# Adding the attention softmax's 1e-9 on ScalarE, as a bias behind the exponentials, instead of on VectorE ahead of the reciprocal

## The chip, the cores and the metric

The kernel runs on one core of a Trainium2 chip. The metric is the time of one execution on the device in microseconds (us); lower is better. The profile comes from one execution of the same program, recorded by the hardware.

## What is computed

Four batches of eight heads of causal attention with a window of 64 positions, then two feed-forward layers. Cut to what matters here:

```python
B, H, S, D = 4, 8, 576, 64
scores = np.where(mask, q @ k.T / np.sqrt(D), -1e9)       # 0 <= row - column < 64
scores = scores - np.max(scores, axis=-1, keepdims=True)
attn = np.exp(scores)
attn = attn / (np.sum(attn, axis=-1, keepdims=True) + 1e-09)
x = attn @ v                       # 2304 tokens x 512
h = x @ w_in                       # 512 x 2048
g = np.where(h >= 1, h, np.where(h <= -1, 0, (h + 1) ** 2 / 4))
x = g @ w_out                      # 2048 x 512
# second layer: h = x @ w_in2 (512 x 1024), h * softmax(h), layer norm, @ w_out2
```

The largest term of every softmax row is exp(0) = 1, so each sum is at least 1.

## The kernel before, in words

**Attention.** The 2304 tokens are cut into 12 tiles of 192 rows, each tile into three blocks of 64 queries that see 128 keys each. A unit of attention is two heads of one tile. The scores of a unit come out of TensorE into PSUM (`st_s`, L352); VectorE adds the mask and takes the maximum (L360); ScalarE makes three exponentials, one for each block, with the maximum as bias and the row sum as accumulator output (L366, each an ACTIVATE with an ACTIVATION_READ_ACCUMULATOR behind it). The three sums of a unit lie side by side in `sm` (128 x 3). `st_norm` adds 1e-9 to them on VectorE, in place (L377), takes the reciprocal into `rs` (L378) and multiplies the 128 x 384 probabilities `p` with it (L386; in a sequence's first tile L382 for the first block and L386 for the other two). `st_t` transposes `p` on TensorE (L400, L402) and ScalarE copies it to SBUF (L405, L407); `st_v` multiplies by v (L421) and splits the result into a high and a low part (`xh` on ScalarE, L428, `xl` on VectorE, L429). The first 18 units are done one at a time like this; the other 30 go in 15 pairs (`pair_s`, `pair_v`), with the same steps under L442, L452, L458, L476, L483 and L484, and `st_norm` is then called twice in a row. In all `st_norm` runs 48 times.

**First layer.** For each of six blocks of 384 tokens there are 16 steps f. A step multiplies `xh` and `xl` with the high and low parts of w_in into `ps_h` (L496, 12 matmuls), applies the activation (`u`: Relu with a bias tile `half` at L505, Square at L506, both ScalarE; L511 VectorE), splits `u` into `gh` (L512, ScalarE) and `gl` (L515, VectorE), and, two steps later, adds the product with w_out to four accumulators (L526, 12 matmuls). `moe_out` copies these out at a block's end (L536 ScalarE, L538 VectorE).

**Weights.** They arrive in HBM as 64-bit numbers. In the first block they are loaded through five staging buffers `wst` (L124, L126; the first ones by SyncE's queue, the others by GpSimd's), and each is turned into a high and a low part in three stages, one per call of `w_conv`: L132 (ScalarE), L136 and L137 (VectorE), L145 (ScalarE) and L146 (VectorE). L146 is the last reader of a staging buffer: the next load waits for it.

**Order.** A main loop runs over the steps f. The attention of later tokens is a generator, `slots()`, from which each step takes one or two pieces; a prologue (ahead of `slots`) does the first seven units by hand. The instructions are not issued in the order in which the program is traced: when the program is built, a planner goes through them with estimated durations and gives each engine, of those that it takes to be ready, the one traced first. On the chip each engine then works through its own queue in that fixed order. A changed instruction can thus move others.

Of the kernel before, what the change touches and what calls it, by code (L numbers as in the profile page):

```python
# [8 lines left out]
F32 = mybir.dt.float32  # L9
F32R = mybir.dt.float32r  # L10
U32 = mybir.dt.uint32
ACTF = mybir.ActivationFunctionType
ALU = mybir.AluOpType
# [7 lines left out]
def kernel(  # L21
# [12 lines left out]
    nc = tc.nc  # L34
# [21 lines left out]
    const = ctx.enter_context(tc.tile_pool(name="const", bufs=1))  # L56
# [8 lines left out]

    make_identity(nc, ident)
    nc.vector.memset(half, 0.5)
    nc.vector.memset(mhalf, -0.5)
    nc.gpsimd.memset(mask, 0.0)
    for x in range(2):  # L70
# [270 lines left out]
    def first(t, i):  # L341
        return t % TPB == 0 and i == 0
# [29 lines left out]
    def st_norm(g, u=None):  # L372
        t = (g if u is None else 2 * g) // NP
        u = g if u is None else (g, u)
        p, sm = pr[u], sums.pop(u)
        rs = at_p.tile([128, QB], F32, tag="rs", name="rs")
        nc.vector.tensor_scalar(sm, sm, 1e-9, None, op0=ALU.add)  # L377
        nc.vector.reciprocal(rs, sm)  # L378
        eng = nc.vector
        i0 = 0  # L380
        if first(t, 0):
            eng.tensor_tensor(  # L382
                p[:, 0, 64:], p[:, 0, 64:], rs[:, 0:1].to_broadcast([128, 64]), op=ALU.mult
            )
            i0 = 1
        eng.tensor_tensor(  # L386
            p[:, i0:, :], p[:, i0:, :],
            rs[:, i0:].rearrange("p (i o) -> p i o", o=1).to_broadcast([128, QB - i0, 128]),
            op=ALU.mult,
        )  # L390
# [172 lines left out]
    for n in range(G0 + 4):  # L563
        if n <= G0:
            st_s(n)
        if 1 <= n <= G0 + 1:
            st_norm(n - 1)
        if 0 <= n - 2 <= G0:
            st_t(n - 2)
        if n == NQ:  # L570
            after(load_qk, 2 * NP)
        if n == NV:
            after(load_v, 2)
        if n + 2 <= G0 + 1:
            st_qkt(n + 2)
        if 0 <= n - 3 < G0:
            st_v(n - 3)
        if n >= NC:
            w_conv()
            w_load(1)  # L580
# [19 lines left out]
    def slots():  # L600
        for g in range(G0 + 1, GB + 1):
            st_s(g)
            yield
            st_v(g - 1)
            st_norm(g)
            yield
            qkt_and_loads(g + 1)
            v_ahead(g)
            yield
            st_t(g)  # L610
            if g == GB:
                st_s(g + 1)
            yield
        st_norm(GB + 1)
        qkt_and_loads(2 * PU)
        yield
# [378 lines left out]
```

## Time and profile before

| | us |
|---|---|
| median of 3 runs | 706.09 (705.32 to 706.83) |
| the profiled execution | 703.17 |
| its span, first to last instruction | 701.4 |
| busy in the span: TensorE matmul, VectorE, ScalarE, GpSimd | 678.1, 448.3, 412.5, 134.2 |

The profile names engines PE (TensorE matmul), PEld (TensorE weight load), DVE (VectorE), ACT (ScalarE), POOL (GpSimd) and SP (SyncE); a q behind the name is that engine's queue of DMA issues. L377 is line 377 of the kernel. An arrow `out<-in` names what is written and what is read. A wait is idle time of the waiting engine, put down to what ended it.

### The profile page before, as it was taken

To read this page: it belongs to the slowest core of one execution; us is meant where nothing else is said; L and a number is where in the kernel's file an instruction comes from. 1 tells how busy PE (TensorE), PEld (TensorE's weight loads), DVE (VectorE), ACT (ScalarE), POOL (GpSimd) and SP (SyncE) were. 2 spreads that over 40 slices of the span, in tenths; PEclk is the share of its full clock that TensorE was granted. 3 is DMA by queue.
4 is the path that set the end of the run, shared out by engine and by line. 5 is a ranking of instruction groups with operands and counts; after the bars stand their busy time and mean duration, and the time that the engine had idled before them with its cause. 6 is when DMAs were issued, how large, how long until landed. Compare 5 with 4: busy or idle time off the path is not lost.

```text
span 701.4 us, 12574 instructions
## 1 busy us (share of the span) xinstructions
PE 678.1 (97%) x4439; PEld 625.6 (89%) x4439; DVE 448.3 (64%) x1213; ACT 412.5 (59%) x1006; POOL 134.2 (19%) x178
## 2 busy tenths in 40 slices
PE   6899888899999999999999999999999999999998
PEld 5689788799999999999999999999997888888887
DVE  4789889646445555454455552643289999999850
ACT  5889777665656655665566565364455555445451
POOL 1112221100001000021112111662272322220000
PEclk9999999999999999999999999999999999999999
DMA  9996896625353523346351211562024455444331
GB/s 194 253 241 161 218 245 196 148 35 108 72 116 112 116 64 76 77 129 126 85 113 61 106 41 51 173 202 93 1 83 142 155 178 189 158 147 150 103 109 46
DMA packets 150551, 88.94 MB, mean 127 GB/s; under 512 B 118616, under 2 KB 134744, under 8 KB 150488
## 3 DMA queue, kind: packets, MB, share of 16 engines
q1 hardware_dynamic: 135160, 49.84, 30.2%
q0 software_dynamic: 12592, 33.57, 14.9%
q10 hardware_dynamic: 2736, 4.72, 1.8%
q8 instruction: 35, 0.57, 0.3%
q14 instruction: 28, 0.23, 0.1%
HBM read 63.97 MB, written 24.12 MB: 126 GB/s over the span
## 4 chain that ended last, share of the span: by engine, by line
PE 71%; issue 13%; POOL 4%; DVE 4%; DMA 3%; SPq 3%; ACT 2%; POOLq 0%; DVEq 0%
PE acc L526 21%; PE ps_h L496 21%; PE ps_o L827 14%; PE P L712 9%; DMA wst<-in_moe_w_in_dram 3%; POOL wil L249 2%; PE ps_x L476 2%; PE ps_s L442 2%; PE ps_p L402 2%; SPq L279 1%; DVE gl L515 1%; POOL wst L124 1%; SPq L302 1%; POOL wst L126 1%; DVE x2p L692 1%
## 5 line engine op out<-in xcount | busy, mean ns | idle before, releaser
L511 DVE SCALAR_TENSOR_TENSOR u<-u,ps_h 128x384 f32<-128x384 f32 (+1 forms) x98 | 53.3, 544 | 142.3 <-ACT u L506 141.4
L496 PE MATMUL ps_h<-xh,wih 128*128 128x384 f32 (+1 forms) x392 | 132.0, 337 | 3.1 <-ACT wih L145 3.0
L526 PE MATMUL acc<-gl,woh 128*128 128x384 f32 (+1 forms) x392 | 130.3, 334 | 2.1 <-DVE gl L515 2.1
L496 PE MATMUL ps_h<-xl,wih 128*128 128x384 f32 (+1 forms) x392 | 130.7, 334 | 0.4 <-DVE xl L429 0.4
L496 PE MATMUL ps_h<-xh,wil 128*128 128x384 f32 (+1 forms) x392 | 130.9, 334 | 0.0
L526 PE MATMUL acc<-gh,wol 128*128 128x384 f32 (+1 forms) x392 | 129.3, 332 | 0.0
L526 PE MATMUL acc<-gh,woh 128*128 128x384 f32 (+1 forms) x392 | 123.8, 341 | 2.3 <-ACT gh L512 2.3
L505 ACT ACTIVATE u<-ps_h,half 128x384 f32<-128x384 f32 (+1 forms) x98 | 56.1, 574 | 97.5 <-PE ps_h L496 97.3
L515 DVE TENSOR_TENSOR gl<-u,gh 128x384 fp32r<-128x384 f32 (+1 forms) x98 | 62.6, 640 | 35.2 <-ACT gh L512 34.6
L512 ACT CAST gh<-u 128x384 fp32r<-128x384 f32 (+1 forms) x98 | 49.7, 508 | 49.9 <-DVE u L511 34.8
L496 PEld LDWEIGHTS ps_h<-xh,wih 128*128 128x128 f32 x392 | 74.1, 189 | 4.5 <-ACT wih L145 3.6
L526 PEld LDWEIGHTS acc<-gh,woh 128*128 128x128 f32 x392 | 72.0, 188 | 6.2 <-ACT gh L512 3.5
L526 PEld LDWEIGHTS acc<-gl,woh 128*128 128x128 f32 x392 | 73.7, 188 | 3.1 <-DVE gl L515 2.7
L496 PEld LDWEIGHTS ps_h<-xl,wih 128*128 128x128 f32 x392 | 74.1, 189 | 1.0 <-DVE xl L429 0.8
L496 PEld LDWEIGHTS ps_h<-xh,wil 128*128 128x128 f32 x392 | 74.1, 189 | 0.1
L526 PEld LDWEIGHTS acc<-gh,wol 128*128 128x128 f32 x392 | 73.6, 188 | 0.1
L712 PE MATMUL P<-wih,x2p 128*128 128x512 f32 x216 | 71.6, 390 | 0.7 <-DVE x2p L692 0.7
L827 PE MATMUL ps_o<-woh,wol 128*128 128x512 f32 (+1 forms) x152 | 57.6, 379 | 0.0
L827 PE MATMUL ps_o<-woh,woh 128*128 128x512 f32 (+1 forms) x152 | 57.5, 379 | 0.0
L827 PE MATMUL ps_o<-wol,woh 128*128 128x512 f32 (+1 forms) x152 | 57.5, 378 | 0.0
L506 ACT ACTIVATE u<-u 128x384 f32<-128x384 f32 (+1 forms) x98 | 51.1, 522 | 1.9
L712 PEld LDWEIGHTS P<-wih,x2p 128*128 128x128 f32 x216 | 40.4, 188 | 9.2 <-DVE x2p L692 1.1
(123 smaller groups left out, 1191.8 us busy)
## 6 DMA issues: line engine op xcount, KB each, us to landing
wst<-in_moe_w_out_dram POOLq DMA_DIRECT2D x22, 512.0 KB, 7.4
wst<-in_moe_w_in_dram POOLq DMA_DIRECT2D x21, 512.0 KB, 5.5
vw<-in_v_dram SPq DMA_DIRECT2D x32, 256.0 KB, 5.3
lnd<-e SPq DMA_DIRECT2D x16, 512.0 KB, 2.7
lT<-lnd SPq DMA_DIRECT2D x64, 128.0 KB, 3.0
x2d<-xo POOLq DMA_DIRECT2D x24, 192.0 KB, 2.6
out_dram<-o ACTq DMA_DIRECT2D x17, 256.0 KB, 2.0
w2d<-w2st POOLq DMA_DIRECT2D x8, 512.0 KB, 3.0
```

Source lines behind the costliest of these rows:

```text
L249: nc.gpsimd.tensor_tensor(lo, v_, as_f32(hi), op=ALU.subtract)
L402: nc.tensor.transpose(ps[:, i * 128:i * 128 + 128], p[:, i, :], ident)
L442: nc.tensor.matmul(ps[x][64 * c:64 * c + 64, i * 128 + c0:i * 128 + 128], z[r, KQ + i * 64:KQ + i * 64 + 64], z[r, i * 64 + c0:i * 64 + 12 ...
L496: nc.tensor.matmul(ps, a, bb[:, kc, c], start=(n == 0), stop=(n == 3 * KC - 1))
L505: nc.scalar.activation(u, ps, ACTF.Relu, bias=half, scale=0.5)
L506: nc.scalar.activation(u, u, ACTF.Square)
L511: g = nc.vector.scalar_tensor_tensor(u, u, 1.0, ps, op0=ALU.min, op1=ALU.max)
L512: return nc.scalar.copy(hi, u).ins, g.ins
L515: nc.vector.tensor_tensor(lo, u, as_f32(hi), op=ALU.subtract)
L526: nc.tensor.matmul(acc[j, e][:, c], a, bb, start=(f == 0 and n == 0 and c.start == 0), stop=(f == NF - 1 and n == 2),)
L712: nc.tensor.matmul(ps, l, r, start=(n == 0), stop=(n == 5))
L827: nc.tensor.matmul(ps, a[kk // 4][:, kk % 4, :], b[kk][:, c:c + w], start=(n == 0), stop=(n == 3 * NK2 - 1),)
```

## The change

A 128 x 1 tile `eps` is filled with 1e-9 by VectorE at the start. In `st_norm`, the addition on VectorE becomes a Relu on ScalarE, in place, with `eps` as bias. The softmax of the second layer (L770) is left as it is.

```diff
     make_identity(nc, ident)
     nc.vector.memset(half, 0.5)
+    eps = const.tile([128, 1], F32, name="eps")
+    nc.vector.memset(eps, 1e-9)
     nc.vector.memset(mhalf, -0.5)
...
         rs = at_p.tile([128, QB], F32, tag="rs", name="rs")
-        nc.vector.tensor_scalar(sm, sm, 1e-9, None, op0=ALU.add)
+        nc.scalar.activation(sm, sm, ACTF.Relu, bias=eps, scale=1.0)
         nc.vector.reciprocal(rs, sm)
```

## Rows read from the trace of the kernel before

**Rows 1.** Busy time by stretch: start and end, length, then PE, PEld, DVE, ACT, POOL.
```profile
0.00:40.00 40.00, 31.67 (x229) 26.72 (x229) 25.26 (x113) 28.29 (x101) 5.31 (x16) 0.96 1.03 221
40.00:140.00 100.00, 90.56 (x652) 84.34 (x652) 84.51 (x247) 76.60 (x201) 18.26 (x29) 1.00 0.80 202
140.00:440.00 300.00, 300.00 (x2322) 290.86 (x2318) 153.41 (x487) 179.77 (x469) 36.03 (x52) 1.00 0.37 89
```

**Rows 2.** The waits of PE up to 140 us: total us, times, longest us.
```profile
PE ps_p L402 <- DVE p L386: 3.7, 2, 2.4
PE ps_h L496 <- ACT wih L145: 3.0, 2, 1.6
...
PE acc L526 <- ACT gh L512: 2.3, 4, 1.3
PE ps_s L352 <- ACT kq L339: 2.0, 4, 1.0
```

**Rows 3.** Busy time by stretch of line 377 alone (x instructions).
```profile
0.00:20.00 20.00, 0.74 (x4) 1.00 1.05 197
20.00:140.00 120.00, 2.29 (x14) 0.99 0.83 209
```

**Rows 4.** Groups of instructions by line and shape: busy us, mean ns of one, idle before.
```profile
L458 ACT ACTIVATE p<-p,mx 128x128 f32<-128x128 f32 x82 | 31.8, 390 | 12.2 <-DVE mx L452 12.2
...
L377 DVE TENSOR_SCALAR sm<-sm 128x3 f32<-128x3 f32 x48 | 7.4, 156 | 2.0 <-ACT p L366 1.2 <-ACT p L458 0.5
...
L458 ACT ACTIVATE p<-p,mx 128x64 f32<-128x64 f32 x8 | 2.7, 342 | 0.2 <-DVE mx L452 0.2
...
L338 ACT ACT_TABLE_LOAD x1 | 1.3, 1283 | 0.7 <-PEq L979 0.7
```

**Rows 5.** Timeline from 31.2 us: start, length, engine, line, operation [idle before <-releaser].
```profile
31.20 0.19 ACT L366 ACTIVATION_READ_ACCUMULATOR p<-p,mx 128x1 f32 x1
...
31.29 0.68 ACT L132 ACTIVATE wst<-wst 128x512 f32<-128x512 f32 x1
...
31.62 0.16 DVE L377 TENSOR_SCALAR sm<-sm 128x3 f32<-128x3 f32 x1
31.82 0.18 DVE L378 RECIPROCAL rs<-sm 128x3 f32<-128x3 f32 x1
...
32.73 0.69 PE L402 MATMUL ps_p<-ident,p 128*128 128x128 f32 x3 [1.37 <-DVE p L386]
```

**Rows 6.** Timeline from 145 us: two dependent instructions of ScalarE.
```profile
145.19 0.58 ACT L505 ACTIVATE u<-ps_h,half 128x384 f32<-128x384 f32 x1 [0.30 <-PE ps_h L496]
...
145.81 0.53 ACT L506 ACTIVATE u<-u 128x384 f32<-128x384 f32 x1
```

**Rows 7.** Waits up to 120 us: GpSimd's weight loads for line 146.
```profile
POOL wst L126 <- DVE wil L146: 23.3, 8, 15.8
```

**Rows 8.** Timeline: a pair's last multiplication, and the first transposes that read the pair.
```profile
145.70 0.56 DVE L386 TENSOR_TENSOR p<-p,rs 128x384 f32<-128x384 f32 x1
...
151.58 0.60 PE L402 MATMUL ps_p<-ident,p 128*128 128x128 f32 x4
```

**Rows 9.** Timeline from 131.8 us.
```profile
131.89 0.19 ACT L366 ACTIVATION_READ_ACCUMULATOR p<-p,mx 128x1 f32 x1
131.98 0.46 ACT L536 COPY xo<-acc 128x384 f32<-128x384 f32 x1
...
132.31 0.17 DVE L378 RECIPROCAL rs<-sm 128x3 f32<-128x3 f32 x1
...
133.23 0.52 PE L402 MATMUL ps_p<-ident,p 128*128 128x128 f32 x3 [2.35 <-DVE p L386]
```

**Rows 10.** The chain that ended last, in order of time: start, us, what.
```profile
20.57 10.68 DMA wst<-in_moe_w_in_dram
```

**Rows 11.** Timeline: one unit of the first block, addition and multiplication.
```profile
73.57 0.16 DVE L377 TENSOR_SCALAR sm<-sm 128x3 f32<-128x3 f32 x1
...
79.91 0.55 DVE L386 TENSOR_TENSOR p<-p,rs 128x384 f32<-128x384 f32 x1
```

## The prediction

> **What bounds the kernel now.** I read the busy times by stretch first. The reader is to see that from 140 to 440 us TensorE is busy for all of its 300 us, while VectorE has 153 and ScalarE 180 [rows 1]: there, nothing that these two do a little sooner or later moves the end. Ahead of 140 us it is not so: TensorE stands still for 8.3 us up to 40 us and for 9.4 us from 40 to 140, and in that second stretch VectorE is busy 85% and ScalarE 77% of the time. So I read the waits of TensorE up to 140 us next [rows 2]. It waits for VectorE's normalized `p` twice (3.7 us in all) and for ScalarE's products (`wih`, `gh`, `kq`) ten times (7.3 us). The change touches the first kind directly, and the second through what it puts into ScalarE's queue. Then I read where the 48 additions lie: 4 up to 20 us, 14 from there to 140 [rows 3], so the other 30, two for each of 15 pairs, lie behind 140 us. The second layer's softmax is not touched, so the end of the kernel is out of reach except by a new order.
>
> **The removed addition.** 48 instructions of 156 ns on VectorE, 7.4 us of busy time [rows 4]. Where the reciprocal follows directly it starts 0.20 us after the addition started (31.62, 31.82) [rows 5]: that is what VectorE gains each time.
>
> **The added Relu.** No row shows an ACTIVATE on three columns, so I bound it. Below: an accumulator read, 0.19 us [rows 5]. Above: the narrowest Exp, 64 columns, 342 ns. That Exp also reads its bias from a 128 x 1 tile, and 64 more columns cost it 390 - 342 = 48 ns [rows 4], so three columns give 342 - 61 x 0.75 = 296 ns, 0.30 us. I take this, since engine, memory and kind of bias are the same. Relu, Exp, Square, Copy and Prelu already run with one table load in the whole trace [rows 4], so no second load comes with it.
>
> **Its wait.** The Relu reads what the third accumulator read has written, on its own engine. An independent instruction starts 0.10 us before such a read ends (31.29 against 31.39) [rows 5], a dependent one 0.04 us after its predecessor's end (145.81 against 145.77) [rows 6]. So the Relu costs ScalarE 0.30 + 0.04 = 0.34 us where nothing fills the gap, as the overlap lost ahead of it is won back behind it; 48 times are 16 us, and they are a price only where ScalarE is late. The reciprocal, which used to follow on VectorE's own queue, now waits across engines. Queued behind it are the multiplication and, in the first block, the weight conversion, and GpSimd's weight loads wait for its last step, L146, 23.3 us in eight waits [rows 7].
>
> **The memset of `eps`.** One instruction of 128 x 1 at the start, ahead of the first transposes' results, when VectorE has nothing to do: nothing. With that cover gone it costs less than an addition, under 0.16 us.
>
> **The 30 units behind 140 us.** Hidden: the pair shown ends its last multiplication at 146.26 and its transposes start at 151.58 [rows 8]; 5.3 us of cover stand against a delay of 0.1 to 0.6 us for each unit, and TensorE is full. Nothing. With the cover gone each would cost what the two places below do.
>
> **Place A, 31 us.** TensorE waits 1.37 us for `p`. The sums are ready at 31.39; VectorE adds at 31.62 and takes the reciprocal at 31.82 [rows 5]. With the Relu first in ScalarE's queue it runs from 31.43 to 31.73, and with 0.04 us of handing over the reciprocal starts at 31.77: 0.05 us earlier. Behind L132, which ends at 31.97 and lets the next start 0.10 us sooner, it runs from 31.87 to 32.17 and the reciprocal starts at 32.21: 0.39 us later. I take the middle, +0.2 us.
>
> **Place B, 132 us.** TensorE waits 2.35 us. Sums ready at 132.08, reciprocal at 132.31 [rows 9]. Relu first: 132.12 to 132.42, reciprocal at 132.46, +0.15 us. Behind the copy L536 (131.98 to 132.44): 132.34 to 132.64, reciprocal at 132.68, +0.37 us. Middle: +0.25 us. From 140 us on TensorE has no idle time to make this up.
>
> **The other 16 early units.** The four up to 20 us hide behind transfers: the chain that ended last runs through a load issued at 20.57 that lands at 31.25 [rows 10]. For the twelve others the addition mostly has no hurry: the one at 73.57 has its multiplication at 79.91 [rows 11], 6.3 us later, since the planner put other work of VectorE between them. So the Relu is done in time, and what is left is occupancy: +0.34 us for ScalarE, -0.20 us for VectorE, each worth something only where that engine is what TensorE or a weight load waits for. Bounds: all twelve on ScalarE's path, +4.1 us; all on VectorE's, -2.4 us. TensorE's waits speak for ScalarE [rows 2], GpSimd's for VectorE [rows 7]; nearly even, so I take +0.2 us.
>
> **Sum.** 0.2 + 0.25 + 0.2 = +0.65 us. The profiled execution took 703.17 us (span 701.4 and 1.77 around it); it would take 703.8. The median of the runs is 2.92 us above the profiled one, and I put the same difference on it: 706.09 + 0.65 = **706.7 us**.
>
> **Rival 1, slower: ScalarE's queue sets the pace of the first 140 us.** The Relu stands in an in-order queue that is 77% busy from 40 to 140 us and for whose products TensorE waits ten times [rows 1, 2]. Each one that lies ahead of an L145, L512 or L339 that is already late costs 0.34 us, and where the planner puts it behind an L132 (0.68 us) the reciprocal and all that VectorE has behind it stand too. With half of the twelve on that path (2.0 us) and A and B at their upper ends (0.39 + 0.37): +2.8 us, **708.9**. It decides once four Relus are on the path (1.4 us). For it: the waits for ScalarE are TensorE's largest. Against it: ScalarE is idle for 23 us of those 100. The Trainium skill (ScalarE: Activation LUTs, section Rules for kernel authors) has this as a rule: Relus and additions belong on VectorE, not on ScalarE. By that rule this rival is the forecast; the trace agrees as far as the single operation goes, and shows for most units that nobody waits for it.
>
> **Rival 2, faster: VectorE sets the pace of the weight conversion.** From 40 to 140 us it is the busiest engine but TensorE [rows 1], and GpSimd's loads wait for its L146 [rows 7]. If each addition taken out brings the loads 0.20 us forward, twelve give 2.4 us; with A at its lower end and B at +0.15 it is -2.3 us, **703.8**. Against it: most of TensorE's waiting is for ScalarE.
>
> **Rival 3: a new order.** The planner sees another engine and other durations, and neighbours in the first 140 us change places; that it interleaves freely there shows in the 6.3 us between an addition and its multiplication [rows 11]. The size is that of one or two waits of TensorE, whose longest are 1.0 to 1.6 us [rows 2], in either direction: 704.5 to 708.9.
>
> **How the numbers follow.** The runs shown spread by 0.2% (1.5 us), so a difference under 0.2%, 1.4 us, can't be told from none. The forecast has 0.46, rival 1 0.24, rival 2 0.12, and rival 3 0.18, which I split into 0.10 slower and 0.08 faster. So faster 0.20, same 0.46, slower 0.34. The forecast's own range is 705.4 to 707.5; the range reaches to rival 1 and most of rival 2 and takes in the bounds of A and B: 704.4 to 709.2.
>
> **What would show it.** Right: 48 Relus of about 0.30 us on `sm` and no addition; the stretch from 140 to 440 us full on TensorE again; the two waits for `p` there and 0.1 to 0.4 us longer; the end of the first block later by under 1.4 us. Rival 1 would show as longer waits of TensorE for `wih`, `gh` and `kq` and new waits of VectorE for `sm`; rival 2 as weight loads that are issued earlier. I would be wrong altogether if the time changed behind 440 us, where no attention is left: that could only come from a new order there.

## The result, and the profile after

The changed kernel takes 708.55 us (median of 9 runs, 706.78 to 711.46), the kernel before took 704.43 beside it (9 runs, 703.57 to 706.83): a ratio of 1.0058, 95% interval 1.0042 to 1.0074. It is slower by 4.1 us, where the prediction had +0.65 and called the time the same. The profiled execution took 708.55 us with a span of 706.8, against 703.17 and 701.4 before. One execution of a kernel told of further down (the waits filled, with the Relu) took 1115.18 us at a mean granted clock of 0.564, where its other eleven had 0.993 to 1.000, and is left out of every figure.

The change itself is there as written. The groups of instructions by line and shape (busy us, mean ns of one, idle before) and the waits of VectorE in the changed kernel, where all lines behind the new two stand two further down (L377 is L379, L386 is L388):

```profile
L379 ACT ACTIVATE sm<-sm,eps 128x3 f32<-128x3 f32 x48 | 12.9, 290 | 0.1
L69 DVE MEMSET eps<- 128x1 f32 x1 | 0.1, 59 | 0.0
DVE rs L380 <- ACT sm L379: 13.9, 17, 1.6
```

48 Relus of 290 ns (0.30 us was estimated), a memset of 59 ns, and a new wait of the reciprocal for ScalarE, 17 times. The busy times by stretch, which answer to [rows 1]:

```profile
0.00:40.00 40.00, 30.95 (x191) 26.43 (x192) 22.82 (x97) 27.63 (x98) 5.29 (x16) 0.92 0.92 223
40.00:140.00 100.00, 91.96 (x646) 86.82 (x646) 83.17 (x241) 76.95 (x211) 18.64 (x29) 0.95 0.74 192
140.00:440.00 300.00, 299.99 (x2325) 289.94 (x2325) 147.90 (x460) 184.72 (x506) 32.38 (x47) 1.00 0.38 90
```

From 140 to 440 us TensorE is as full as before, so what was lost was lost ahead of that. But TensorE does not stand still longer in the first 140 us: 9.05 + 8.04 = 17.1 us, against 8.3 + 9.4 = 17.7 before. Its waits there, which answer to [rows 2], first those for what the two engines make:

```profile
PE ps_p L404 <- DVE p L388: 4.1, 3, 2.1
PE ps_p L404 <- ACT woh L147: 2.8, 1, 2.8
PE ps_s L354 <- ACT kq L341: 2.0, 3, 1.3
PE ps_h L498 <- DVE xl L431: 1.6, 2, 1.1
PE acc L528 <- ACT gh L514: 1.2, 2, 0.6
```

The waits of `ps_p` for the normalized `p` have grown from 3.7 us to 6.9, with a new one of 2.8 at 52 us. The waits for `wih` (3.0 us before) are gone: with TensorE later, the weights are in time. So the sum of the waits hides the loss. What shows it is the sixth number behind the length in the same view by 10 us, the clock that TensorE was granted (1.00 is 2.4 GHz, 0.50 is 1.2). The kernel before:

```profile
30.00:40.00 10.00, 8.54 (x82) 7.51 (x81) 8.01 (x26) 9.07 (x31) 1.84 (x3) 0.83 0.88 169
40.00:50.00 10.00, 9.01 (x89) 8.41 (x88) 8.16 (x32) 8.80 (x30) 1.31 (x2) 1.00 1.05 272
50.00:60.00 10.00, 10.00 (x77) 9.72 (x77) 9.28 (x27) 9.47 (x26) 2.06 (x3) 1.00 0.56 166
130.00:140.00 10.00, 7.61 (x71) 6.61 (x71) 6.54 (x25) 5.87 (x21) 2.17 (x5) 1.00 0.94 234
```

The changed kernel:

```profile
30.00:40.00 10.00, 7.25 (x50) 6.21 (x51) 8.37 (x27) 8.59 (x26) 1.84 (x3) 0.69 0.77 163
40.00:50.00 10.00, 9.23 (x92) 8.57 (x91) 8.18 (x29) 7.54 (x22) 1.30 (x2) 0.96 0.85 249
50.00:60.00 10.00, 6.69 (x41) 6.00 (x40) 9.54 (x27) 9.49 (x29) 2.87 (x4) 0.66 0.87 241
130.00:140.00 10.00, 7.20 (x48) 6.55 (x47) 5.96 (x26) 4.92 (x22) 2.71 (x5) 0.83 0.65 166
```

A mean of 0.83 over 10 us is a third of it at half clock. In the trace, TensorE ran at half clock for 3.4 us before (32.9 to 36.4), and for 6.8 (33.9 to 40.7), 6.8 (51.0 to 57.8) and 3.4 us (136.3 to 139.7) after. Before, the stretch lies behind the first of the two waits for `p`, and none behind the longer second. After, the first and the third begin inside a wait for `p`; the second begins 1.0 us ahead of the wait of 2.8 us, behind waits of 0.8 and 0.5 us. What a stretch costs is read from TensorE's own rows at the two levels, start and length, in the changed kernel:

```profile
34.08 0.88 PE L404 MATMUL ps_p<-ident,p 128*128 128x128 f32 x3 [1.68 <-DVE p L388]
36.27 0.41 PE L498 MATMUL ps_h<-xh,wil 128*128 128x192 f32 x1
36.48 0.42 PE L498 MATMUL ps_h<-xh,wih 128*128 128x192 f32 x1
41.20 0.28 PE L498 MATMUL ps_h<-xl,wih 128*128 128x192 f32 x1
41.31 0.28 PE L498 MATMUL ps_h<-xh,wil 128*128 128x192 f32 x1
```

At half clock these matmuls start 0.21 us apart, at full clock 0.11. So half of TensorE's busy time in such a stretch is lost. Two more things had changed. The order that the planner gives is another: place by place in the two traces, and with the moved operation left out, TensorE's queue names another instruction at 556 places, VectorE's at 267 and ScalarE's at 211, the first at 17 us. And a new wait stands at 52 us, in unit 8 (units are numbered from 0 in the order of the work; place A of the prediction is unit 6, place B unit 16). ScalarE and VectorE there, in the changed kernel:

```profile
50.81 0.20 ACT L368 ACTIVATION_READ_ACCUMULATOR p<-p,mx 128x1 f32 x1
50.91 0.68 ACT L134 ACTIVATE wst<-wst 128x512 f32<-128x512 f32 x1
51.48 0.67 ACT L147 CAST wih<-wst 128x512 fp32r<-128x512 f32 x1
52.02 0.32 ACT L379 ACTIVATE sm<-sm,eps 128x3 f32<-128x3 f32 x1
...
52.50 0.68 DVE L148 TENSOR_TENSOR wil<-wst,wih 128x512 fp32r<-128x512 f32 x1
53.10 0.16 DVE L380 RECIPROCAL rs<-sm 128x3 f32<-128x3 f32 x1
53.19 0.65 DVE L139 SCALAR_TENSOR_TENSOR wst<-wst 128x512 uint32<-128x512 uint32 x1
53.77 0.41 DVE L138 TENSOR_SCALAR wst<-wst 128x512 uint32<-128x512 uint32 x1
54.10 0.54 DVE L388 TENSOR_TENSOR p<-p,rs 128x384 f32<-128x384 f32 x1
```

The sums are ready at 51.01. The Relu stands behind two conversions and runs from 52.02 to 52.34; the reciprocal stands behind VectorE's own conversion L148, which ends at 53.18; `p` is ready at 54.64, and the transposes, which had waited since 51.99, start at 54.79. The profile names `woh` (L147) as what ended this wait, since that instruction ended at 54.80; it is `p`.

### The profile page after: what moved, and what is told of

It is laid out like the page before. It is cut to its first block, busy times and chain, and to the rows that moved or that the text cites. A ratio compares the mean times of both kernels' runs of the same rounds, so it can differ in the third digit from the quotient of the medians.

```text
span 706.8 us, 12558 instructions
## 1 busy us (share of the span) xinstructions
PE 684.3 (97%) x4439; PEld 632.5 (89%) x4439; DVE 440.5 (62%) x1166; ACT 420.1 (59%) x1054; POOL 134.5 (19%) x178
## 5 line engine op out<-in xcount | busy, mean ns | idle before, releaser
L528 PE MATMUL acc<-gh,woh 128*128 128x384 f32 (+1 forms) x392 | 128.4, 342 | 1.2 <-ACT gh L514 1.2
L514 ACT CAST gh<-u 128x384 fp32r<-128x384 f32 (+1 forms) x98 | 49.7, 509 | 49.3 <-DVE u L513 33.9
```

Source lines behind the costliest of these rows:

```text
L514: return nc.scalar.copy(hi, u).ins, g.ins
L528: nc.tensor.matmul(acc[j, e][:, c], a, bb, start=(f == 0 and n == 0 and c.start == 0), stop=(f == NF - 1 and n == 2),)
```

## The experiments

Three things were mixed: the Relu, the order, and the clock. To part them, an order can be fixed: a function ties each engine's instructions one behind the other, in an order taken from one of the two kernels.

```diff
+def pin_order(tc):
+    want = json.loads(zlib.decompress(base64.b85decode(_ORDER)))
...
+        for a, b in zip(order, order[1:]):
+            tc.add_manual_dep(b, a.name, info, reason="order")
```

**Relu in the order of before** (each Relu directly behind its third Exp).

```diff
+        pin_order(tc)
```

> The changed kernel's instructions, but each engine's queue tied to the order that it has in the kernel before; each Relu stands directly behind its unit's third exponential. Theory A (the planner's new order makes the loss): ratio to the kernel before 0.999 to 1.002, the stretch at half the TensorE clock near 51 us and the one near 136 us are gone, and the only half-clock stretch ahead of 600 us is the one near 33 us, 3.4 us long. Theory B (the Relu itself makes it, by its 0.29 us on ScalarE and the handing over to VectorE): ratio 1.004 to 1.008, as the change measured. Theory C (both about evenly): 1.002 to 1.004.

Measured: 708.82 us (6 runs, 707.96 to 710.57), ratio 1.0064 [1.0048, 1.0080].

**The add in the order of after** (the kernel before, each add directly ahead of its reciprocal).

```diff
+        pin_order(tc)
```

> The mirror image: the kernel before with its addition on VectorE, but each queue tied to the order that it has in the changed kernel, the addition directly ahead of its reciprocal. Theory A: ratio 1.004 to 1.008, with TensorE waiting 2 to 3 us for the transposes near 52 us and near 135 us and the clock at half behind each. Theory B: 0.998 to 1.002. Theory C: 1.002 to 1.004.

Measured: 709.21 us (6 runs, 708.88 to 710.21), ratio 1.0070 [1.0055, 1.0084]. Unit 8 in this kernel, VectorE and then TensorE:

```profile
52.33 0.68 DVE L146 TENSOR_TENSOR wil<-wst,wih 128x512 fp32r<-128x512 f32 x1
52.93 0.15 DVE L377 TENSOR_SCALAR sm<-sm 128x3 f32<-128x3 f32 x1
53.12 0.18 DVE L378 RECIPROCAL rs<-sm 128x3 f32<-128x3 f32 x1
...
54.82 0.87 PE L402 MATMUL ps_p<-ident,p 128*128 128x128 f32 x3 [3.43 <-DVE p L386]
```

The sums are ready at 50.85, but the add and the reciprocal stand behind the same conversion, and TensorE waits 3.43 us without any Relu, against 2.80 with it. So the wait at unit 8 comes from the place of these instructions in VectorE's queue, that is, from the new order; the Relu's 1.0 us behind ScalarE's conversions cost nothing there. The half clock comes with the order too: 10.2 us from 31.3, 6.8 from 51.8 and 3.4 from 137.1 us.

**The Relu in the first 18 units only**, order left to the planner.

```diff
-        nc.scalar.activation(sm, sm, ACTF.Relu, bias=eps, scale=1.0)
+        if not isinstance(u, tuple):
+            nc.scalar.activation(sm, sm, ACTF.Relu, bias=eps, scale=1.0)
+        else:
+            nc.vector.tensor_scalar(sm, sm, 1e-9, None, op0=ALU.add)
```

> The Relu in the 18 units that are done one at a time, the addition on VectorE in the 15 pairs; order left to the planner. All theories put the loss ahead of 150 us: ratio 1.004 to 1.007, the lag against the kernel before 4 to 5 us at 150 us and unchanged from there. If the 30 units behind 150 us carry a share by themselves, the ratio is under 1.003.

Measured: 708.50 us (6 runs, 707.53 to 709.90), ratio 1.0057 [1.0042, 1.0073].

**The Relu in the 15 pairs only**: the same edit with the two branches exchanged.

> The Relu in the 15 pairs alone, the addition on VectorE in the first 18 units; order left to the planner. Expected ratio 0.999 to 1.002: hidden under a full TensorE from 140 to 440 us, at most the 0.5 us that the changed kernel loses near 400 us. Over 1.003 would say that the prediction's cover for these units does not hold.

Measured: 704.18 us (12 runs, 702.22 to 708.18), ratio 0.9990 [0.9973, 1.0006].

What follows: the pairs are hidden, and the whole loss comes from the first 18 units. But the Relu without the new order loses 0.64%, the new order without the Relu 0.70%, and both together 0.58%: they don't add up, so neither is a price by itself. In the order of before, place by place, the two traces show it. The waits at A and B are nearly those of before, 1.34 us (1.37) and 2.48 us (2.35), but the lag behind the kernel before grows by 1.6 us at 23 to 25 us, by 1.2 behind A and by 3.4 at B (0.8 of that in a wait for the next unit's products, which before did not have). TensorE at B in this kernel, against 0.52 us for the transposes and 0.83 for the scores at the same place before:

```profile
136.21 0.87 PE L404 MATMUL ps_p<-ident,p 128*128 128x128 f32 x3 [2.48 <-DVE p L388]
136.88 1.49 PE L354 MATMUL ps_s<-kq 128*128 128x128 f32 x6
```

And at 23 us, where both kernels have waited 0.4 us, the kernel before:

```profile
22.77 0.94 PE L352 MATMUL ps_s<-kq 128*128 128x128 f32 x6 [0.38 <-ACT kq L339]
23.54 0.27 PE L400 MATMUL ps_p<-ident,p 128*64 128x128 f32 x1
```

and the Relu in the same order:

```profile
22.79 1.65 PE L354 MATMUL ps_s<-kq 128*128 128x128 f32 x6 [0.37 <-ACT kq L341]
24.23 0.42 PE L402 MATMUL ps_p<-ident,p 128*64 128x128 f32 x1
```

The same work starts at the same time and takes 0.7 us more. TensorE begins every profiled execution at half clock; the trace has no clock record for this (the column prints 1.00), but the matmuls show it. They run at full clock from 22.7 us on before, from 26.4 here, from 27.1 in the changed kernel. That is not the Relu's doing alone: see the last section.

From the traces I added up, up to the 501st product matmul of the first layer (`acc`, at 256.7 us before): TensorE's idle time, and its busy time at half clock, the start included. Half of the latter is the loss:

| kernel | starts at | idle | busy at half clock | half of it | the rest |
|---|---|---|---|---|---|
| before | 256.7 | 17.8 | 20.2 | 10.1 | 228.8 |
| after | 261.7 | 17.1 | 34.5 | 17.2 | 227.3 |
| Relu, old order | 263.1 | 18.5 | 31.6 | 15.8 | 228.7 |
| add, new order | 262.0 | 20.7 | 24.1 | 12.0 | 229.3 |
| Relu in singles | 261.7 | 16.1 | 36.3 | 18.2 | 227.4 |
| Relu in pairs | 259.3 | 17.3 | 25.9 | 12.9 | 229.1 |

The rest agrees within 2 us over all six. So in the profiled executions it is the half clock that tells the three slow Relu kernels from the one before (+5.7 to +8.1 us), not the idle time (-1.7 to +0.7); only the add in the new order has more idle time as well (+2.9). Part of this is the start, which varies by itself (last section); behind the start, the loss at half clock is 1.7 us before and 5.6 to 8.5 in the four slow kernels. The granted clock of every execution is on record too, its start apart. Its mean is 0.992 to 0.994 in the kernel before (17 to 35 executions beside each experiment), 0.991 with the Relu in the old order (6), but 0.987 in the changed kernel (9) and 0.986 with the add in the new order (6): the lower clock goes with the new order, with or without the Relu. But such a table can take company for cause. The **clock theory** says that the loss is TensorE's speed behind its waits for `p`; its rival, that it is the lateness of `p` itself. The next runs take the half clock away and leave `p` as late as it is.

**The waits filled, with the Relu and with the add, in the order of before.** Matmuls whose product nobody reads stand ahead of the transposes, in the unused last quarter of the same bank:

```diff
+FILL = {('p', 6): 5, ('p', 16): 9}
...
+    def fillers(site, ps):
+        for _ in range(FILL.get(site, 0)):
+            i = nc.tensor.matmul(ps[:, 384:512], ident, ident, start=True, stop=True)
+            FILLERS.add(i.ins.name)
...
         ps = at_bank("ps_p")
+        fillers(("p", u), ps)
         o = at_p.tile([128, QB, 128], F32, tag="pT", name="pT")
```

> relu_old_order (Relu on ScalarE, every engine in the order of before) with matmuls that nobody reads (ident by ident, 128 columns, into the unused last quarter of the bank) on TensorE directly ahead of the transposes that wait for p: 5 in unit 6 (the wait of 1.34 us at 33 us) and 9 in unit 16 (2.48 us at 134 us). Of the 6.3 us that relu_old_order lost by its profile, about 4.6 came behind these two waits, where the granted clock stood at 0.5 for 6.83 us each. Clock theory: the waits are filled, the clock stays at full speed behind them, and most of those 4.6 us come back: ratio to before 0.998 to 1.002 (703.5 to 706.0 us). Rival, the wait for p itself: p comes no earlier, the loss stays: ratio 1.004 to 1.008 (707.5 to 710 us).

> The kernel before in its own order with the same 5 and 9 unread matmuls ahead of the same two waits. Clock theory: before has one half-clock stretch of 3.41 us behind the first wait in its profile, and its runs spread over 4 us, so some of that comes back: ratio 0.996 to 1.000. Against relu_fill_waits it says how much of Relu against add is left once both waits are filled: at most 0.5 us of difference by the clock theory (the 0.2 us by which p comes later, twice), 4 us by the rival, which expects 1.000 here.

Measured: the Relu 704.64 us (11 runs, 703.50 to 705.67), ratio 0.9989 [0.9973, 1.0005], down from 1.0064 without the fillers. The add 702.73 us (12 runs, 700.36 to 704.91), ratio 0.9962 [0.9946, 0.9978], faster than either kernel. TensorE at A and B with the Relu, and the stretches around them:

```profile
33.32 1.38 PE L315 MATMUL ps_p<-ident 128*128 128x128 f32 x10
34.59 0.52 PE L412 MATMUL ps_p<-ident,p 128*128 128x128 f32 x3
...
132.82 1.84 PE L315 MATMUL ps_p<-ident 128*128 128x128 f32 x15
134.69 0.52 PE L412 MATMUL ps_p<-ident,p 128*128 128x128 f32 x3
135.05 0.83 PE L361 MATMUL ps_s<-kq 128*128 128x128 f32 x6
```

```profile
30.00:40.00 10.00, 8.95 (x92) 7.55 (x91) 8.89 (x31) 9.90 (x34) 1.56 (x3) 1.00 0.89 158
130.00:140.00 10.00, 8.98 (x79) 7.99 (x78) 5.35 (x22) 5.47 (x21) 2.72 (x5) 1.00 0.91 223
```

`p` is ready 1.13 us after its sums, as without the fillers; the transposes take 0.52 us in place of 0.87, the clock stays at 1.00 in these stretches (in this profile it is at half from 20.9 to 27.7 and from 92.5 to 95.9 us), and the ratio falls by 0.75%. That is the clock theory's number. Its other one was missed: the Relu still stands 1.9 us above the add, not 0.5. For the same fillers take 0.38% off the add as well. So of the 0.64% by which the Relu is slower than the add in this order, 0.27% is left when the waits are filled in both; somewhat over half, 0.37%, went with the speed behind A and B, though the intervals make this split a rough one.

**The start filled too.**

```diff
-FILL = {('p', 6): 5, ('p', 16): 9}
+FILL = {('t', 0): 2, ('t', 1): 2, ('s', 1): 3, ('s', 3): 1, ('p', 6): 5, ('p', 16): 9}
```

> relu_fill_waits with unread matmuls ahead of the first waits for data too: 2 ahead of the first transposes of units 0 and 1, 3 ahead of the scores of unit 1 and 1 ahead of those of unit 3 (idle stretches of TensorE of 2.75, 0.58, 1.24 and 0.65 us up to 14.3 us). In relu_old_order the matmuls run at the pitch of the half clock until 26.4 us, in before until 22.7 us. Clock theory: the full clock comes earlier and 1.5 to 4 us more come back: 700 to 704 us, ratio 0.993 to 0.999. Rival: matmuls that nobody reads only add work: 1.004 or more.

Measured: 704.13 us (12 runs, 703.17 to 705.13), ratio 0.9983 [0.9971, 0.9995]. The full clock came at 7.9 us, but fell again for 3.4 us at 18, and TensorE now waited 1.3 us for the scores' operands at 12 us: 0.5 us gained on the Relu with A and B filled, 1.5 to 4 expected.

**No addition at all**, in the order of before; the 1e-9 is left out.

```diff
-        nc.vector.tensor_scalar(sm, sm, 1e-9, None, op0=ALU.add)
```

> The order of before, with no addition at all: neither VectorE nor ScalarE adds the 1e-9 (left out of the computation). It shows what the 48 adds of before cost, that is the most that moving them could have brought, and whether taking 0.2 us from the way to p does as much good as adding 0.1 to 0.2 us did harm. Waits alone: 0.2 us at each of the two places, 0.3 to 0.6 us in all: ratio 0.9990 to 1.0000. Clock theory: the same, or up to 2 us better where a half-clock stretch falls away: 0.997 to 1.0000.

Measured: 704.82 us (12 runs, 702.14 to 706.72), ratio 0.9987 [0.9972, 1.0002]. All 48 adds together cost at most 2 us, likely 0.9, and perhaps nothing. That is the most that moving them could have brought in this order. The profile of this kernel has 6.8 us of half clock at A and 3.4 at B, more than that of the kernel before, though nothing was added and its executions have the same mean granted clock (0.993): a warning about single profiles.

**The changed kernel in its own order, with its waits filled.**

```diff
+FILL = {('p', 6): 6, ('p', 8): 9, ('p', 16): 8}
```

> The changed kernel, its own order on every engine, with unread matmuls on TensorE directly ahead of the transposes of the three units that wait long for p in its profile: 6 in unit 6 (1.68 us at 32 us), 9 in unit 8 (2.80 us at 52 us), 8 in unit 16 (2.12 us at 135 us); the granted clock stood at 0.5 for 6.83, 6.83 and 3.41 us there. Clock theory: half of those 17 us, less what later waits for weights take back, is the change's loss: ratio 0.998 to 1.002 (704 to 706.5 us) in place of 1.0058. Rival, the order and the later p themselves: 1.005 or more (708 us).

Measured: 709.24 us (6 runs, 707.75 to 711.09), ratio 1.0061 [1.0037, 1.0085]: no gain. But in this order it is unit 5 that waits at 32 us. Its wait stayed, the half clock there too, and the six fillers of unit 6 ran in that. The half clock at 51 and 136 us (10.2 us without fillers) is gone from this profile, and still the time is no shorter:

```profile
39.47 2.52 PE L315 MATMUL ps_p<-ident 128*128 128x128 f32 x12
41.82 0.49 PE L412 MATMUL ps_p<-ident,p 128*128 128x128 f32 x3
```

**The same with unit 5.**

```diff
-FILL = {('p', 6): 6, ('p', 8): 9, ('p', 16): 8}
+FILL = {('p', 5): 6, ('p', 8): 9, ('p', 16): 8}
```

> after_fill_waits with its first 6 unread matmuls ahead of unit 5 in place of unit 6: in the order of the changed kernel it is unit 5 whose transposes wait 1.7 us for p at 32 us, unit 6 does not wait, and there the 6 ran at half clock and only took 2.5 us (39.47 to 41.82 us). Clock theory: those 2.5 us fall away, and with the wait filled the half clock behind it too (6.83 us, worth up to 3.4): 709.24 less 2.5 to 5.9, 703.3 to 706.7 us, ratio 0.998 to 1.002. Rival (in this order p and the weights come late whatever the clock, and TensorE only waits longer elsewhere): no less than 707.5 us, 1.004 or more; between the two, both are at work.

Measured: 707.56 us (12 runs, 705.91 to 708.50), ratio 1.0029 [1.0015, 1.0042], against 1.0058 [1.0042, 1.0074] without fillers. From 24.6 us on the clock never falls, so here it can be seen what the new order costs without it. TensorE's waits from 55 to 80 us in this kernel:

```profile
PE ps_p L412 <- ACT kq L347: 1.3, 1, 1.3
PE ps_h L506 <- DVE u L521: 0.6, 1, 0.6
PE acc L536 <- ACT gh L522: 0.6, 1, 0.6
```

At 57 us this kernel is 2.7 us ahead of the changed one; at 89 us it is level with it. The lead went into these 2.5 us of waits for ScalarE and VectorE, of which the changed kernel has only 0.6: its half clock had covered the others.

It would be natural to say that half of the change's loss, 0.29% of 0.58%, is the clock. But its fair partner is the kernel before with its own waits filled, and that is at 0.9962. Against it the changed kernel is slower by 0.67%, 4.8 us, no less than the 0.58% without fillers on either side; and the mean granted clock is the same in these two, 0.997 (12 executions each, the start apart). So with this half clock taken from both, the change costs what it cost before. For this order the rival of the clock theory is borne out: what makes the changed kernel slower is that its operands come late, and the half clock mostly stood in the place of waits. At the same clock the Relu in the order of before costs 0.27%. So about 0.4% comes with the new order and about 0.3% with the Relu itself; the fillers stand at other units in the two orders and the chips differ, so these two shares are rough.

**Two more, for a better version**: the add in the order of before, with the waits for weights filled, and with the start too.

```diff
+FILL = {('p', 6): 5, ('p', 16): 9, ('h', 0, 6, 0): 5, ('h', 0, 8, 0): 7}
```

> add_fill_waits (add on VectorE, waits for p filled in units 6 and 16) with 5 and 7 unread matmuls ahead of the two waits for weights at 78 and 89 us too (1.36 and 1.85 us); behind the second its profile had the clock at 0.5 for 3.41 us. Clock theory: that stretch falls away, but the next wait for weights at 114 us takes up to 0.9 us of it: 0.3 to 1.2 us under add_fill_waits, ratio 0.994 to 0.997. Rival (TensorE waits there for weights whatever its clock): no change, 0.996.

```diff
+FILL = {('t', 0): 2, ('t', 1): 2, ('s', 1): 3, ('s', 3): 1, ('p', 6): 5, ('p', 16): 9, ('h', 0, 6, 0): 5, ('h', 0, 8, 0): 7}
```

> add_fill_weights with the unread matmuls ahead of the first waits for data of relu_fill_start as well (2, 2, 3, 1 up to 14 us). With the Relu these brought 0.7 us, since VectorE and ScalarE became what is waited for up to 30 us. Expected 0 to 1.5 us under add_fill_weights, ratio 0.992 to 0.997; a rival by which earlier matmuls only lead to longer waits, and so to half clock at other places, gives 0.997 to 1.000.

Measured: 703.37 us (12 runs, 700.88 to 705.62), 0.9978 [0.9962, 0.9993], and 702.15 us (12 runs, 700.19 to 705.11), 0.9958 [0.9941, 0.9975]. The first tested little: its five ran at 66 us, where TensorE didn't wait, its seven at 78, and the wait at 89 us stayed, with its 3.4 us of half clock. The second is the fastest kernel here, though not by more than the intervals of the one with A and B filled alone.

## Why the prediction was right and wrong

The time, 708.55 us, lies in the range; the call "same" was wrong, and the sum with it.

- **The Relu's price** (0.30 us) and **the memset** (under 0.16): right, 0.290 and 0.059 us.
- **The 30 units behind 140 us** at nothing: right, 0.9990 [0.9973, 1.0006] with the Relu in these alone.
- **A new order** had no term in the sum; it stood among the rivals alone. This is the step that failed: the sum prices the Relu at its places in the order of before, but the planner's new order alone, with the add, costs 0.70%, and with the waits filled in both kernels the change costs 0.67%, where the Relu in the order of before costs 0.27%.
- **Places A and B**: as delays, right. In the order of before, with the Relu first in the queue, the forecast was 0.05 us earlier at A and 0.15 later at B; the waits are 1.34 and 2.48 us, 0.03 shorter and 0.13 longer. As prices, too small: +0.2 and +0.25 us took the wait for the whole cost, and left out the speed at which TensorE goes on behind it. In the profile the lag grew by 1.2 us behind A and by 3.4 around B, with the granted clock at 0.5 for 6.8 us at each; with the waits filled in both kernels, what the Relu costs in this order fell from 0.64% to 0.27%. That rest, 1.9 us, is still more than the whole sum of 0.65, and no run shows where it lies. In the changed kernel's own order these two delays do not occur as forecast: unit 5 waits 1.68 us in place of unit 6, and unit 16 waits 2.12 us, less than before.
- **The other early units**: +0.2 us was too small as well. Unit 8 alone has a new wait of 2.8 us. It is rival 3's, not rival 1's: the add waits 3.43 us there in the same order. The forecast had placed these units by one that nobody waits for [rows 11].
- **The end of the first block**, forecast under 1.4 us later, is 2.8 us later: ScalarE's copy L536 of [rows 9], at 131.98 us before, starts at 134.73.
- **The four units up to 20 us** at nothing: not settled. In the profiled executions the start at half clock lasted 3.7 and 4.4 us longer with the Relu, but it varies by more than that from one execution to the next (last section).
- **Rival 1** had the size (708.9), but by luck: it counts Relus on ScalarE's path, and the wait where a Relu does stand behind conversions is as long with the add. Of its signs the new waits of VectorE for `sm` came, but not longer waits for `wih` and `gh`, which fell, likely since a later TensorE finds them ready. The Trainium skill (ScalarE: Activation LUTs, section Rules for kernel authors) keeps Relus and additions on VectorE. That rule gives the right sign in the order of before, and the single operation agrees: 290 ns on ScalarE against 156 [rows 4].
- **Rival 2** had its cause in VectorE's relief. Leaving the adds out altogether gives 0.9987 [0.9972, 1.0002], so there was next to nothing to win.
- **Rival 3**, a new order, is what the runs show: alone it costs 0.70% (709.21 us, just above its bound of 708.9), and in unit 8 the sums then stand behind VectorE's conversions. Its bound was taken from waits of 1.0 to 1.6 us, though [rows 2] has one of 2.4 for `p`, the kind that the new order made longer.
- **The bound of 0.2%** was taken from three runs of before. Nine runs spread from 703.57 to 706.83, 0.5%; of that the comparison by many runs resolves 0.15% to 0.2%.

## What to carry to other kernels

Where TensorE is the bound, price a wait of it by the granted clock around it as well as by its length, and look for stretches at half clock before and after a change by short windows, since the sum of the waits can fall while the time rises. But a shorter half clock is not yet a shorter kernel: take it away from the kernel before as well, and compare those two. When an edit moves other instructions, run the new order with the old operation before blaming the operation: in unit 8 the Relu stood 1.0 us behind conversions and TensorE waited 2.8 us, but with the add in that order it waited 3.4. And measure what leaving the operation out would bring before moving it: here 0.13% in the order of before.

## What was not expected of the hardware

The granted clock fell to 0.5 around waits of only 0.4 to 3.4 us, on a TensorE that was busy around them, and stayed there for 3.4, 6.8 or 10.2 us. The same wait does not always have the same effect: 1.37 us at A was followed by 3.4 us of half clock before, 1.34 us by 6.8 with the Relu. And the kernel with the Relu in the pairs alone, whose early part is that of before, has no half clock behind A in its profile, but some around 50 and at 135 us, where the kernel before had none:

```profile
30.00:40.00 10.00, 8.42 (x89) 7.36 (x90) 9.44 (x32) 9.96 (x34) 1.84 (x3) 1.00 0.62 144
40.00:50.00 10.00, 8.64 (x81) 7.91 (x81) 8.27 (x31) 8.94 (x29) 1.30 (x2) 0.94 1.21 268
50.00:60.00 10.00, 10.00 (x67) 9.96 (x66) 7.30 (x20) 7.51 (x18) 2.06 (x3) 0.89 0.50 167
130.00:140.00 10.00, 7.64 (x60) 7.03 (x59) 5.63 (x23) 4.63 (x18) 2.73 (x5) 0.83 0.85 221
```

The start differs as much. The Relu in the order of before with and without fillers at A and B is one program up to 32 us, and its full clock came at 14.0 us in the one profile, to fall again from 20.9 to 27.7, and at 26.4 in the other. The Trainium skill (TensorE: Matmul & The Clock Gate, Part 1) says that the number of slow matmuls at a start differs from run to run of one kernel; these two agree. This likely makes much of the 3 us by which the nine runs of before differ, and it is why a single profile can't say what an edit costs in clock, and only many runs can. What decides whether a given wait is followed by half clock stays open here. The matmuls that nobody reads took 2.5 us of TensorE where they were put at the wrong unit; at the right two they gained 0.4% on a kernel that had nothing else changed.
